# Top-32 attention and two MLPs on one core: soft-masked tiles by one VectorE pass and a ScalarE copy, the third visit on the batch's scales, another order table

## The chip, the cores and the metric

The kernel runs on one core of a Trainium2 chip. The metric is device time in microseconds of one execution, the median of several runs. The core's engines run side by side, each in its own fixed order of instructions: TensorE (PE in the profile, its weight loads PEld), VectorE (DVE), ScalarE (ACT), GpSimd (POOL) and SyncE (SP), which here issues every DMA.

## The reference

Four batches of eight heads, 576 rows, 64 columns. Attention keeps, in each row of scores, only those that are at least the 32nd largest. What comes out is laid as 2304 tokens of 512 and goes through two MLPs of 512 to 2048 to 512, the first with softplus, the second with `h - tanh(h)`.

```python
scores = scale * np.matmul(q, k.transpose(0, 1, 3, 2))
kth = np.partition(scores, -top_k, axis=-1)[..., -top_k:-top_k + 1]      # top_k = 32
scores = np.where(scores >= kth, scores, -1000000000.0)
scores = scores - np.max(scores, axis=-1, keepdims=True)
attn = np.exp(scores)
attn = attn / (np.sum(attn, axis=-1, keepdims=True) + 1e-09)
x = np.matmul(attn, v)                        # laid as 2304 x 512
g = np.maximum(h, 0.0) + np.log1p(np.exp(-np.abs(h)))   # h = x @ w_in;  x = g @ w_out
g = h - np.tanh(h)                                      # h = x @ w_in2; out = g @ w_out2
```

The inputs are float32 (moe_w_in and moe_w_out come as pairs of 32-bit words, which the kernel reads as 64-bit numbers and converts itself).

## The kernel before

**Tiles and visits.** A visit is one batch, one pair of heads and two of the four blocks of 128 query rows: four tiles of 128x576 scores. Sixteen of the 32 visits also carry a small tile with the 64 rows left over of each of the two heads, which gives 144 tiles in all. Each tile goes this way: `front` multiplies q by k on TensorE (tile name s) and ScalarE copies the scores to SBUF (ssb); `chain` finds the 32 largest by four MAX8 and three MATCH_REPLACE8 on VectorE (m, x); `exps` makes the exponentials on ScalarE; `mask`; `turn` splits the result in two f16 parts (ScalarE casts hl, GpSimd subtracts for the lower part) and transposes them by DMA (pT); `back` multiplies by v on TensorE (px), and ScalarE, VectorE and GpSimd divide by the sum (r2) and split the output (x, xs), which a DMA transposes into the MLP's input (xy). Two or three tiles' worth of buffers are there for each.

**Two ways to the exponential.** Where ScalarE holds the softplus table because the first MLP is in work, a tile is "soft": `exps` takes softplus in place of the exponential, and `mask` sets what lies under the threshold to zero. There are 59 such tiles. The other 85 take a Prelu and an Exp, which mask by themselves, and `mask` does nothing. With SOFT at 1 a soft tile's mask is a VectorE comparison into ssb (1 or 0 times 2^38) and a GpSimd product of x and ssb.

**Scales.** All operands are split into f16 pairs after a scaling by a power of two that follows from a sum of squares. The q and k of a batch are scaled by sums over the whole batch (`qk_norm`, called for batch 0 as part of tile 4's loop turn), which `visit_scales` hands out. The first OWN visits don't wait for that: `visit_norm` takes their own sums from the q and k just loaded (tile name qss), with two ScalarE squares, two one-column products on TensorE and some small VectorE operations. A visit that comes again to the same heads finds its k in a saved copy; where that copy was scaled by the visit's own sum, three more one-element VectorE operations follow.

**MLPs.** A chunk is 256 tokens (128 for the rows left over). `gemm1` multiplies by w_in (h), `act1` applies softplus or tanh on ScalarE (r) and splits the result (g; ScalarE and GpSimd), `gemm2` multiplies by w_out (y). The weights are loaded, converted and split in 32 groups during the first quarter of the run, on all engines (whi, wlo, xy as staging).

**What sets the order.** Nothing is issued while the code runs: a `Recorder` takes down every operation with a cost in ns (`price`) and what it depends on. `order` then plans: `place` is a list scheduler over the five engines with a rank for every operation, in ns; `order` starts from the program's order with a random addition (SEED, SIG), plans five times, each time with ranks from the latest starts of the plan before, and keeps the plan with the earliest end. DLAT is what the planner adds to every DMA. `idle` puts filler matmuls of 256 columns (line 564) into gaps of TensorE's plan. `run` issues all operations in the planned order, from line 567, so nearly every row of the profile has that line and is told apart by its tile.

Of the kernel before, what the change touches and what calls it, by code (L numbers as in the profile page):

```python
# [33 lines left out]
NRM = 'cccc'  # L34
EVL = 'AA'
HIC = 'AAAA'
SOFT = 1
NKT = 3
NM = 3
NQT = 2  # L40
# [2 lines left out]
RSE = 1  # L43
KE = 'P'
NQH = 1
OWN = 3
OWN0 = 0
V0 = 0
EXQ = 0
# [24 lines left out]
LT = 1  # L74
NBF = 1
NJ = 0
SEED = 34
DLAT = 1100
MRX = 60.0
LAGA = 3  # L80
LAGB = 4
# [38 lines left out]
MARGD = 0.0  # L120
MARGA = 0.0
MARGP = 0.0


class View:
# [48 lines left out]
class Recorder:  # L174
# [199 lines left out]
    def place(self, edges, count, rank, margin, ring):  # L374
# [14 lines left out]
        while True:  # L389
# [67 lines left out]
            if ring and e == "SP":  # L457
                busy = max(busy, t + 800) + o.lat
                end[i] = busy + DLAT
            for j, lat in edges[i]:  # L460
# [7 lines left out]
    def order(self, margin):  # L468

        ops = self.ops  # L470
        succ = self.link()
        self.lead = [self.shared(o) for o in ops]
        rank = [o.rank for o in ops]
        if SEED:
            draw = random.Random(SEED)
            rank = [r + draw.gauss(0.0, SIG) for r in rank]
        best = None
        for turn in range(TURNS):
            start, end, done = self.place(succ, [len(o.preds) for o in ops], rank, margin, True)
            total = max(start[o.i] + o.cost for o in ops)  # L480
            if best is None or total < best[0]:
                best = total, done, start, end
            back = [[] for _ in ops]
            for o in ops:
                for j, lat in o.preds.items():
                    back[o.i].append((j, lat + (end[j] - start[j] - ops[j].cost if ops[j].eng == "SP" else 0.0)))
            late = self.place(back, [len(x) for x in succ], [-x for x in start], {}, False)[1]
            rank = [-x for x in late]
        for o in ops:
            o.start = best[2][o.i]  # L490
        self.ends = best[3]
        return best[1]

    def idle(self, done):

# [75 lines left out]
def topk_attention_two_mlps(  # L571
# [388 lines left out]
    def visit_norm(vi):  # L960

        pair = tiny(2), tiny(2)
        (vi.sq, vi.sk), (vi.iq, vi.ik) = ([t[:, u : u + 1] for u in range(2)] for t in pair)
        vi.es, vi.nes, vi.nst = (tiny() for _ in range(3))
        both = NJ and vi.again is None
        ss = al("qss", 1, [P, 3], F32)
        left = vi.left is not None
        if vi.again is not None:
            vi.sk, vi.ik = None, vi.again[2]
        if left:  # L970
            j, st = xy_take([P, D], F16, "nst")
            xy_free.append(j)
            nc.scalar.activation(st, vi.ql, AF.Square, accum_out=ss[:, 1:2])
        for u, (t, s, inv) in enumerate(((vi.q, vi.sq, vi.iq), (vi.k, vi.sk, vi.ik))):
            if t is None:
                continue
            j, st = xy_take([P, 2 * D * t.shape[2]], F16, "nst")
            xy_free.append(j)
            nc.scalar.activation(st, t.rearrange("p j t d -> p (j t d)"), AF.Square, accum_out=ss[:, 2 * u : 2 * u + 1])
            n = 2 if u == 0 and left else 1  # L980
            if not both:
                pow2_scale(col_norm(ss[:, 2 * u : 2 * u + n], n), s, inv)
        if both:
            pow2_scale(col_norms([ss[:, 0 : 2 if left else 1], ss[:, 2:3]]), *pair)
        exp_scale(vi.iq, vi.ik, vi.es, vi.nes, vi.nst)
# [286 lines left out]
    def mask(st):  # L1272
        if st.soft and SOFT:
            nc.vector.tensor_scalar(st.s, st.s, st.m[:, 31:32], PUP, op0=ALU.is_ge, op1=ALU.mult)
            nc.gpsimd.tensor_mul(st.p, st.p, st.s)
        elif st.soft:
            nc.vector.scalar_tensor_tensor(st.p, st.s, st.m[:, 31:32], st.p, op0=ALU.is_ge, op1=ALU.mult)
            nc.scalar.activation(st.p, st.p, AF.Copy, scale=PUP)
# [193 lines left out]
    def run_gemm2(stp):  # L1472
        ch = stp.ch
        if stp.g == 0:
            acc = new_acc(ch.T)
            if stp.m == 0:
                ch.acc1 = acc
            else:
                ch.acc2 = acc
        stp.acc = ch.acc1 if stp.m == 0 else ch.acc2  # L1480
        gemm2(stp)
        if stp.g == NG - 1:
            if stp.m == 0:
                y_finish(ch)
            else:
                out_finish(ch)
# [104 lines left out]
    def prep_for(st):  # L1591
# [3 lines left out]
        if not vi.kT:  # L1595
            if i < OWN or OWN0 and vi.b == 0:
                visit_norm(vi)
# [48 lines left out]
    def next_step(n):  # L1646

        if phase[0] is None:
            can1 = c1[0] < len(order) and order[c1[0]][1] <= n
            can2 = wdone[0] == 4 * NG and c1[0] >= MINC  # L1650
            if can2 and len(kept) >= AHEAD:
                phase[0] = (kept.pop(0), 1)
            elif can1:
                ch = order[c1[0]][0]
                c1[0] += 1
                kept.append(ch)
                phase[0] = (ch, 0)
            elif can2 and kept:
                phase[0] = (kept.pop(0), 1)
            else:  # L1660
                return None
            phase[1] = 0
        (ch, m), g = phase
        phase[1] += 1
        if phase[1] == NG:
            phase[0] = None
        return ch, m, g
# [118 lines left out]
    while pend:  # L1786
        run_gemm2(pend.pop(0))
    nc.run(tc, {"PE": MARG, "DVE": MARGD, "ACT": MARGA, "POOL": MARGP})

# [29 lines left out]
```

## Time and profile before

| | |
|---|---|
| median of 3 runs | 1158.74 us (1156.74 to 1159.31) |
| the profiled execution's own time | 1160.61 us |
| its span | 1158.9 us |
| PE busy | 1015.5 us (88% of the span) |
| DVE busy | 960.0 us (83%) |
| ACT busy | 908.6 us (78%) |
| POOL busy | 870.9 us (75%) |

The page cuts the span into 40 slices. DVE's busy share is eight or nine tenths in all slices from the second to the 34th, and then falls away; PE's is between two and seven tenths in the first seven and eight or nine tenths after them, to the end. PE's granted clock is under nine tenths of full speed in the second to the eighth slice. So the two engines that carry most of the work are not short of it at the same time: the one has little to do at the end, the other at the start.

### The profile page before, as it was taken

What the parts mean: (1) busy time and instruction counts of PE and PEld (TensorE: products, weight loads), DVE (VectorE), ACT (ScalarE), POOL (GpSimd) and SP (SyncE); (2) the same over time, 40 slices, a digit from 0 to 9 for tenths busy, and PEclk for the clock granted to TensorE, in tenths of its full rate; (3) what the DMA queues carried; (4) which work ended last, traced back from release to release, by engine and by line L of the source; (5) the groups of instructions that cost most, each with busy time, mean ns of one, the idle gap of its engine ahead of it and who ended that gap; (6) DMA issues with size and microseconds to landing.
All of it is one profiled execution on the core that took longest, in us unless ns stands there. A gap on an engine that the chain in (4) does not pass through costs nothing.

```text
span 1158.9 us, 27885 instructions
## 1 busy us (share of the span) xinstructions
PE 1015.5 (88%) x9979; PEld 787.2 (68%) x9979; DVE 960.0 (83%) x2116; ACT 908.6 (78%) x1891; POOL 870.9 (75%) x1234
## 2 busy tenths in 40 slices
PE   4377542898898989999999999999998999999998
PEld 2244331687657867887689867886687779977965
DVE  4989999999998999989999999999899999510111
ACT  7899999899997988778877987798678776733422
POOL 5456899899887967967899879888796699543433
PEclk9688855899999999999999999999999999999999
DMA  9988977935689785655764754557555353200000
GB/s 308 248 268 250 274 209 211 205 104 88 128 176 221 161 181 104 147 81 108 148 149 86 154 96 105 112 105 145 125 99 132 81 107 69 48 6 19 2 9 20
DMA packets 322828, 153.17 MB, mean 132 GB/s; under 512 B 270208, under 2 KB 302464, under 8 KB 322688
## 3 DMA queue, kind: packets, MB, share of 16 engines
q1 hardware_dynamic: 322688, 151.39, 57.2%
q8 instruction: 78, 1.28, 0.5%
q14 instruction: 62, 0.51, 0.1%
HBM read 73.04 MB, written 15.37 MB: 76 GB/s over the span
## 4 chain that ended last, share of the span: by engine, by line
PE 42%; ACT 15%; POOL 13%; DVE 13%; DMA 8%; issue 7%; SPq 1%; POOLq 0%; ACTq 0%; DVEq 0%
PE y L567 19%; PE h L567 18%; DVE m L567 5%; DVE x L567 4%; POOL hl L567 4%; PE px L567 3%; ACT x L567 2%; PE s L567 2%; DMA pT<-hl 2%; POOL g L567 2%; ACT whi L567 2%; ACT ssb L567 2%; ACT r L567 2%; ACT hl L567 1%; ACT xy L567 1%
## 5 line engine op out<-in xcount | busy, mean ns | idle before, releaser
L567 PEld LDWEIGHTS <-whi 128*128 128x128 f16 x3872 | 359.5, 98 | 80.7 <-issue 23.7
L567 PE MATMUL h<-xy,whi 128*128 128x256 f16 (+1 forms) x2560 | 395.9, 263 | 10.6 <-ACT r L567 6.4
L567 PE MATMUL h<-xy,wlo 128*128 128x256 f16 (+1 forms) x1280 | 324.8, 263 | 0.0
L567 DVE MAX8 m<-x 128x8 f32<-128x576 f32 x432 | 315.2, 746 | 1.2
L567 POOL TENSOR_TENSOR hl<-x,hl 128x64 f16<-128x64 f32 (+1 forms) x288 | 214.8, 763 | 54.9 <-ACT hl L567 47.0
L567 DVE MATCH_REPLACE8 x<-m,x 128x576 f32<-128x576 f32 x288 | 212.9, 740 | 0.0
L567 PEld LDWEIGHTS <-wlo 128*128 128x128 f16 x1920 | 188.0, 98 | 21.6 <-issue 3.7
L567 PE MATMUL y<-g,whi 128*128 128x256 f16 (+1 forms) x1280 | 200.1, 262 | 1.6 <-POOL g L567 1.3
L567 PE MATMUL y<-whi,g 128*128 128x512 f16 x576 | 195.5, 380 | 0.2
L567 POOL TENSOR_TENSOR g<-r,g 128x512 f16<-128x512 f32 (+1 forms) x160 | 172.0, 1076 | 13.4 <-PE y L567 8.4
L567 PE MATMUL y<-g,wlo 128*128 128x256 f16 (+1 forms) x640 | 163.0, 262 | 0.0
L567 DVE SCALAR_TENSOR_TENSOR r<-h,hinb,r 128x512 f32<-128x512 f32 (+1 forms) x80 | 55.0, 688 | 119.5 <-ACT r L567 119.3
L567 ACT ACTIVATE x<-ssb,nb,tiny 128x576 f32<-128x576 f32 x144 | 124.4, 866 | 23.0 <-DVE m L567 16.4
L567 PEld LDWEIGHTS <-g 128*128 128x128 f16 x864 | 81.9, 98 | 72.8 <-issue 1.3
L567 PEld LDWEIGHTS <-pT 128*128 128x128 f16 (+1 forms) x2240 | 89.9, 103 | 43.6 <-issue 21.6
L567 DVE MAX8 m<-ssb 128x8 f32<-128x576 f32 x144 | 107.6, 747 | 13.8 <-ACT ssb L567 13.4
L567 PE MATMUL px<-vhl,pT 128*128 128x65 f16 (+1 forms) x2240 | 97.1, 198 | 20.3 <-DMA pT<-hl 6.7
L567 ACT CAST hl<-x 128x576 f16<-128x576 f32 x144 | 96.3, 669 | 22.1 <-POOL x L567 19.6
L567 PE MATMUL s<-kT,qT 128*128 128x288 f16 x512 | 89.1, 299 | 24.8 <-ACT ssb L567 22.8
L567 PE MATMUL y<-wlo,g 128*128 128x512 f16 x288 | 109.2, 379 | 0.0
L567 DVE MATCH_REPLACE8 x<-m,ssb 128x576 f32<-128x576 f32 x144 | 106.5, 739 | 0.0
L567 POOL TENSOR_SCALAR r<-r,gsb 128x512 f32<-128x512 f32 (+1 forms) x80 | 53.5, 669 | 59.1 <-ACT g L567 58.5
(129 smaller groups left out, 1788.8 us busy)
## 6 DMA issues: line engine op xcount, KB each, us to landing
whi<-in_moe_w_in_dram SPq DMA_DIRECT2D x8, 1024.0 KB, 5.8
wlo<-in_moe_w_in_dram SPq DMA_DIRECT2D x6, 1024.0 KB, 7.4
vd<-vhl SPq DMA_DIRECT2D x16, 330.0 KB, 3.7
vhl<-vd SPq DMA_DIRECT2D x16, 330.0 KB, 3.6
kd<-kT SPq DMA_DIRECT2D x32, 160.0 KB, 2.4
whi<-in_moe_w_out_dram SPq DMA_DIRECT2D x5, 1024.0 KB, 5.5
wlo<-in_moe_w_out_dram SPq DMA_DIRECT2D x5, 1024.0 KB, 6.3
kT<-kd SPq DMA_DIRECT2D x32, 160.0 KB, 2.7
```

The lines of the kernel that those rows point to most:

```text
L567: fn(*a, **k)
```

## The change

Three numbers and the planner's last step change. SOFT at 0 takes the other branch of `mask`, which stood in the code before: one VectorE operation compares the scores with the threshold and multiplies x by the result, and a ScalarE copy with a scale of 2^38 follows in place. OWN at 2 lets the third visit take the batch's scales. SEED and DLAT get other values, and after the five plans a table of 51 entries is applied: each adds a random number (its seed, its spread) to the rank of the operations that the kept plan starts in a stretch (from, to, in ns of the plan); the sum is planned once more and issued.

```diff
-SOFT = 1
+SOFT = 0
-OWN = 3
+OWN = 2
-SEED = 34
-DLAT = 1100
+SEED = 3
+DLAT = 1700
+SHIFTS = (
+    (51873, 627410, 687410, 400), (80903, 645783, 665783, 150), (38871, 414678, 434678, 400), (11372, 845916, 865916, 150),
...
+)
             late = self.place(back, [len(x) for x in succ], [-x for x in start], {}, False)[1]
             rank = [-x for x in late]
+        home = list(best[2])
+        rank = list(home)
+        for seed, lo, hi, sigma in SHIFTS:
+            draw = random.Random(seed)
+            rank = [r + (draw.gauss(0.0, sigma) if lo <= h < hi else 0.0) for r, h in zip(rank, home)]
+        start, self.ends, done = self.place(succ, [len(o.preds) for o in ops], rank, margin, True)
         for o in ops:
-            o.start = best[2][o.i]
-        self.ends = best[3]
-        return best[1]
+            o.start = start[o.i]
+        return done
```

Every engine's order differs from the first instructions on. Counted over the whole program, the number of instructions changes only so: DVE's 59 comparisons become 59 products, and 12 one-column operations go; POOL loses 59 products; ACT gets 59 copies and loses two squares; PE loses two one-column products and has 111 filler matmuls where there were 87 (41 ahead of the first MLP product where there were 56, 70 behind it where there were 31). The instructions of the new kernel have line 588 (fillers 585).

On SyncE, around the transposes that bring the first chunk's input (xy_0_80 from xs_130 is its last part). Before:

```order
L567 DMA_TRANSPOSE pT_123<-hl_122 128x9x128
L567 DMA_TRANSPOSE pT_126<-hl_125 128x9x128
L567 DMA vhl_133<-vd_134 128x1320
L567 DMA whi_0_71<-in_moe_w_out_dram 128x512 x2
L567 DMA_TRANSPOSE xy_0_80<-xs_127 128x2x128
L567 DMA whi_0_71<-in_moe_w_out_dram 128x512 x2
L567 DMA_TRANSPOSE pT_123<-hl_122 128x9x128
L567 DMA xy_0_98<-in_moe_w_out_dram 128x512
L567 DMA_TRANSPOSE xy_0_80<-xs_130 128x2x128
```

And now:

```order
L588 DMA_TRANSPOSE pT_123<-hl_122 128x9x128
L588 DMA_TRANSPOSE qlT_145<-zq_63 128x4x128
L588 DMA ql_140<-in_q_dram 64x64
L588 DMA_TRANSPOSE pT_126<-hl_125 128x9x128
L588 DMA_TRANSPOSE xy_0_80<-xs_127 128x2x128
L588 DMA xy_0_113<-in_moe_w_out_dram 128x512
L588 DMA xy_0_98<-in_moe_w_out_dram 128x512
L588 DMA whi_0_71<-in_moe_w_out_dram 128x512 x2
L588 DMA_TRANSPOSE xy_0_80<-xs_130 128x2x128
```

A later tile's pT transpose, which stood between the two xy transposes, stands behind them now; the weight loads ahead of them are others, in about the same number.

On GpSimd, at the first soft tiles. Before:

```order
L567 TENSOR_TENSOR x_111<-x_111,ssb_96 128x576
L567 MEMSET kraw_73 64x2x64
L567 TENSOR_SCALAR nb_124<-m_94,tiny_64 128x1
L567 TENSOR_TENSOR zq_63<-ql_140,zq_63 64x128 x2
L567 TENSOR_TENSOR x_121<-x_121,ssb_112 128x576
L567 TENSOR_TENSOR hl_125<-x_111,hl_125 128x512
L567 TENSOR_TENSOR hl_125<-x_111,hl_125 128x64
```

And now:

```order
L588 TENSOR_SCALAR nb_124<-m_94,tiny_64 128x1
L588 TENSOR_TENSOR wlo_0_72<-whi_0_71 128x512 x2
L588 TENSOR_TENSOR hl_122<-x_95,hl_122 128x64
L588 TENSOR_TENSOR hl_122<-x_95,hl_122 128x512
L588 TENSOR_TENSOR hl_125<-x_111,hl_125 128x64
L588 TENSOR_TENSOR hl_125<-x_111,hl_125 128x512
L588 TENSOR_SCALAR nb_119<-m_110,tiny_64 128x1
```

The products of x and ssb are gone, and the subtractions for hl follow each other with less between them.

On ScalarE, at the first soft tile (x_95). Before, around its cast:

```order
L567 CAST xs_127<-x_0_128 128x128
L567 COPY ssb_93<-s_92 128x576
L567 ACTIVATE x_1_131<-px_78,r_0_129 128x64
L567 ACTIVATE wlo_0_72<-wlo_0_72 128x256 x2
L567 ACTIVATE wlo_0_72<-wlo_0_72,tiny_64 128x256
L567 CAST hl_122<-x_95 128x576
L567 ACTIVATE r_1_132<-px_78,tiny_64 128x1
```

And now, around the new copy:

```order
L588 ACTIVATE px_81,ss_109<-px_81 128x128
L588 ACTIVATE wlo_0_72<-wlo_0_72,tiny_64 128x256
L588 ACTIVATE x_95<-x_95 128x576
L588 ACTIVATE wlo_0_72<-wlo_0_72,tiny_64 128x256
L588 ACTIVATE r_2_136<-px_78,tiny_64 128x1
L588 COPY ssb_93<-s_92 128x576
```

The copy of x_95 stands between two weight conversions and ahead of a step of another tile's `back` (r_2_136); the cast of the same tile follows later on ScalarE.

## Rows read from the trace of the kernel before

**Rows 1.** Four stretches: busy us (instructions) by engine, PE's clock, DMA.
```profile
core 0: us, PE busy (x) PEld busy (x) DVE busy (x) ACT busy (x) POOL busy (x), PEclk, DMA share, GB/s
0.00:223.00 223.00, 116.07 (x750) 72.55 (x751) 202.11 (x450) 206.52 (x432) 161.26 (x204) 0.73 0.90 251
223.00:450.00 227.00, 205.65 (x2046) 163.54 (x2043) 213.93 (x482) 208.81 (x469) 189.07 (x277) 0.98 0.71 149
450.00:1000.00 550.00, 539.44 (x5822) 434.18 (x5820) 523.94 (x1147) 434.83 (x894) 459.25 (x674) 1.00 0.54 111
1000.00:1159.00 159.00, 154.38 (x1372) 116.96 (x1369) 20.04 (x40) 58.47 (x98) 61.35 (x81) 1.00 0.06 16
```

**Rows 2.** Timeline of PE at the first MLP product: start, us, instruction, [idle before].
```profile
220.59 0.39 PE L567 MATMUL px<-whi,tiny 128*128 128x128 bf16 x2 [1.06 <-DVE whi L567]
...
223.03 0.38 PE L567 MATMUL h<-xy,whi 128*128 128x256 f16 x2
```

**Rows 3.** Timeline of SyncE's queue: the last transpose of the first chunk's input.
```profile
218.53 1.17 SPq L567 DMA_TRANSPOSE xy<-xs x1
```

**Rows 4.** DMA issues from 218.4 to 219.8 us: us from issue to landing last.
```profile
xy<-xs SPq DMA_TRANSPOSE x1, 5.0
```

**Rows 5.** Timeline of GpSimd, 195 to 222 us.
```profile
206.43 2.38 POOL L567 TENSOR_TENSOR x<-x,ssb 128x576 f32<-128x576 f32 x1
...
215.63 0.60 POOL L567 TENSOR_TENSOR xs<-x,xs 128x128 f16<-128x128 f32 x1
```

**Rows 6.** Groups by form: count | busy us, mean ns | idle just before, releaser.
```profile
L567 POOL TENSOR_TENSOR x<-x,ssb 128x576 f32<-128x576 f32 x59 | 85.2, 1444 | 6.0 <-DVE ssb L567 5.4
L567 DVE TENSOR_SCALAR ssb<-ssb,m 128x576 f32<-128x576 f32 x59 | 49.4, 840 | 4.1 <-ACT x L567 4.0
L567 ACT CAST hl<-x 128x576 f16<-128x576 f32 x144 | 96.3, 669 | 22.1 <-POOL x L567 19.6 <-DMA pT<-hl 1.9
L567 ACT COPY ssb<-s 128x576 f32<-128x576 f32 x144 | 91.3, 634 | 5.1 <-PE s L567 3.3 <-POOL x L567 1.0
```

**Rows 7.** Tiles ssb, vhl and xy on DVE: duration ns min/median/max, first and last start.
```profile
L567 DVE TENSOR_SCALAR ssb<-ssb,m x59: 496/636/2695, 203.7 to 981.2; 128x576 f32<-128x576 f32 x59
L567 DVE SCALAR_TENSOR_TENSOR vhl<-v,tiny,vhl x16: 857/877/2010, 29.3 to 879.5; 128x640 f16<-128x640 f32 x16
L567 DVE SCALAR_TENSOR_TENSOR xy<-xy x36: 399/494/1377, 58.9 to 273.4; 128x256 int32<-128x256 int32 x36
```

**Rows 8.** Group by form: the two-input pass over vhl.
```profile
L567 DVE SCALAR_TENSOR_TENSOR vhl<-v,tiny,vhl 128x640 f16<-128x640 f32 x16 | 16.6, 1036 | 2.7 <-ACT vhl L567 2.7
```

**Rows 9.** GpSimd's products of x and ssb by stretch: busy us (count), clock, DMA.
```profile
0.00:223.00 223.00, 5.18 (x3) 0.73 0.90 251
223.00:450.00 227.00, 16.30 (x11) 0.98 0.71 149
450.00:1000.00 550.00, 63.73 (x45) 1.00 0.54 111
```

**Rows 10.** Waits from 223 to 450 us: who, for whom, us in total, times, longest.
```profile
PEld L567 <- DMA pT<-hl: 7.1, 9, 1.9
PE h L567 <- ACT r L567: 5.8, 4, 2.8
PE px L567 <- DMA pT<-hl: 3.6, 5, 1.6
```

**Rows 11.** Timeline of PE: the last one-column product of batch 0's norms.
```profile
70.23 0.16 PE L567 MATMUL px<-tiny 128*128 128x1 bf16 x1 [0.56 <-ACT x L567]
```

**Rows 12.** Timeline of ACT, 80 to 92 us: the third visit's k.
```profile
83.52 0.72 ACT L567 ACTIVATE xy<-kraw 128x640 f16<-128x640 f32 x1
...
89.69 0.55 ACT L567 ACTIVATE khl<-kraw,tiny 128x320 f16<-128x320 f32 x1
```

**Rows 13.** Groups: the filler matmuls.
```profile
L564 PE MATMUL y<-tiny 128*128 128x256 bf16 x56 | 8.7, 311 | 0.0
L564 PE MATMUL h<-tiny 128*128 128x256 bf16 x31 | 4.8, 274 | 0.0
```

12 rows, old and new, of the table SHIFTS are left out of this document.

## The prediction

> **What bounds the kernel now.** I read the time by stretches first [rows 1]. From 450 to 1000 us PE is busy for 539.4 of 550 us and from 1000 on for 154.4 of 159, at full clock (1.00, the 2.4 GHz level): there it is full. DVE has nearly nothing left after 1000 us (20 of 159). Ahead of 223 us it is the other way round: DVE is busy for 202 of 223 us, ACT for 206.5, PE for 116. The reader is to see that 223 us is no arbitrary cut: the first product of the MLPs starts at 223.03 [rows 2], and from there PE is the bound, with 227 - 205.65 = 21.35 us of idle time to 450, 550 - 539.44 = 10.56 to 1000 and 159 - 154.38 = 4.62 behind it, the last of it for the output. So the span is
>
> 223.0 (start of the MLPs) + 899.5 (PE's work after it: 205.65 + 539.44 + 154.38) + 36.5 (its idle time) = 1159.0.
>
> None of the edits takes work from the 899.5. The time can only move by the start, by the 36.5 us of idle time and by what is added to PE.
>
> What sets the start: the last transposed part of the first chunk's input is issued at 218.53 [rows 3] and lands 5.0 us later [rows 4], as the product starts. It had waited for its split on POOL at 215.63 [rows 5]. PE's own wait of 1.06 us at 220.59, for a weight [rows 2], lies ahead of the landing and is covered.
>
> **The change, part by part.**
>
> *The masks.* For each of 59 soft tiles POOL loses 1.44 us and DVE's comparison of 0.84 us goes [rows 6]. The comparison lasted 0.50 us at its shortest, 0.64 in the middle [rows 7]: the mean is made of waiting. In its place DVE gets a pass over x, scores and threshold. No row shows it with 576 elements. Of the same operation, 256 elements took 0.399 and 640 took 0.857 us at their shortest [rows 7], which puts 576 at 0.78 (0.399 + 320 x 0.458 / 384); the mean of the second lies 0.18 above its shortest [rows 8], so with such waits 0.96. I take 0.90, between them, bounds 0.77 (0.857 x 576 / 640) and 1.18 (0.84 with the old wait of 0.34 on top): +0.06 us a tile, 3.5 in all, between -4 and +20. ACT gets a copy; the cast of as many elements takes 0.67, the copy of the scores 0.63 [rows 6]. I take 0.65, 38 us in all; nearest rows on both sides leave it between 0.55 and 0.80.
>
> Per tile the chain from the threshold to the cast gets shorter, from 0.84 + 1.44 to 0.90 + 0.65, by 0.73 us, and POOL is free for 1.44 us. Where does that count? Three masks lie ahead of 223 us, 11 between 223 and 450, 45 later [rows 9]. In the middle stretch PE and its weight loads waited 3.6 + 7.1 us for transposed tiles [rows 10]; some third of that stretch's tiles are soft (11 of about 34 casts), so 3 to 4 us of those waits can go. ACT loses there 227 - 208.8 = 18.2 us of slack [rows 1] only to 11 x 0.65 = 7.2. After 450 ACT has 115 us of slack for 45 x 0.65 = 29, and its waits of 19.6 us for POOL's product [rows 6] go.
>
> The skill has a rule that speaks against this part. The Trainium skill, SBUF — State Buffer, "Who interferes with whom": a VectorE instruction with two SBUF inputs shares a read interface with a GpSimd instruction that reads SBUF, and the second to start blocks until the first is through. By that rule the new pass gets no less lock time than the comparison, though it uses no double-port mode; the 2.01 us maximum of the two-input pass [rows 7] agrees.
>
> *The third visit.* Its own squares (0.72 us on ACT for k, at 83.52, and a shorter one for q), two one-column products on PE and 12 one-column DVE operations go, some 2 us on two engines that are both nearly full at that time. The new wait is for batch 0's scales. Their last one-column product ran at 70.23 [rows 11]; the visit's first cast of k stood at 89.69, 6.2 us behind the square [rows 12]. Behind it on ACT are the next casts and the copies of scores, which DVE waits for. With 19 us to spare the wait is hidden. If that cover went, each us of delay would go onto the start.
>
> *The order.* Read from the order: ahead of the split that ends the first chunk, POOL has one product of x and ssb less (the one of 2.38 us [rows 5]); DVE has 17 instructions less ahead of the sixteenth tile's reciprocal; SyncE has 182 rows ahead of the last xy transpose where it had 181. So DVE, POOL and PE have less ahead of the first product and the DMA queue has as much. Start: -2 us. Bounds: -4 (POOL's 2.38 and the third visit's 2 in full), +1 (a landing that takes longer behind four weight loads).
>
> The rest of the order I can't price by rows. Coarsely it is the same: the first MLP products stand behind 18 tiles' `back` products where they stood behind 19, and at no later place are they more than some 6 us of PE work apart. The planner gains nothing in PE's work; what it can gain is in the 36.5 us. Idle time from 223 to 450: -3, the waits for transposes from above; bounds -10 (half of it) and +7 (the ACT copies in full). From 450 to 1000: -1.5 of 10.56; bounds -5 and +5. Tail: 0.
>
> *Fillers.* 24 more. A filler took 13.5/87 = 0.155 us of busy time [rows 13], 3.7 us in all, nearly all inside gaps: +0.5, bounds 0 and 3.7.
>
> Sum: -2 - 3 - 1.5 + 0 + 0.5 = -6. The profiled execution took 1160.61 us, 1.7 more than its span and 1.9 more than the median; -6 gives 1154.6 for it and 1152.7 beside the median of 1158.74. I predict 1153.
>
> **The rivals.**
>
> *A. ScalarE becomes the bound in the middle stretch (slower).* Place: 223 to 450 us, where it is busy for 92% and grows to 95%. PE already waits 5.8 us there for softplus and tanh results (r) [rows 10]. If every copy stands ahead of such a result, PE waits 7.2 us more, the 3 us gained on transposes are lost, and the planner's shorter start gives back 2: 1158.7 + 7.2 - 2 + 0.5 = 1164. It decides from the point where that wait passes 5.8 + 5 = 11 us. For it: ACT is the fullest engine ahead of 223 us. Against: a product stands on PE well ahead of its use, since `gemm2` lags three steps behind. 17%.
>
> *B. The fillers tell of new holes (slower).* The planner fills only stretches that it finds mostly empty. Behind the first MLP product it now places 70 where there were 31: 21 around the 49th tile's products (8 before), 7 around the 69th (none), 12 near the last tiles (3). PE's longest single wait of the middle stretch was 2.8 us [rows 10]; three holes of that size are +8.4, the result 1158.7 + 8.4 - 6 = 1161. Against: DLAT adds 600 ns to each planned DMA, and the holes may be made of that alone. 9%.
>
> *C. DVE's pass is longer than I take it (no change).* With the full lock time it lasts up to 1.18 us; at 1.07, halfway to that from 0.96, it costs +0.23 x 14 = 3.2 us ahead of 450 us and 0.23 x 45 = 10 after, against 26 us of slack there (550 - 523.9), of which I put 3 on PE. 1152.7 + 6.2 = 1159. The rule above is this rival's: by it, lock time stays; the rows show it in some passes only. 14%.
>
> *D. The order table takes much of the idle time (faster by far).* Half of 21.35 and of 10.56, with a start 6 us earlier: 1158.7 - 16 - 6 = 1137. For it: the waits are many and short, which is what moving instructions can cure. Against: the ranks were moved within a plan of modelled costs, and DVE is busy for 95% from 450 to 1000, so that there is little room to move. 14%.
>
> **How the numbers follow.** My forecast, 1147 to 1156, has 46%; A 17, B 9, C 14, D 14. Two runs of this kernel can't tell less than 0.2%, 2.3 us, from no change. Faster by over 2.3 us: the forecast and D, 60%. Within: C and what B misses, 16%. Slower: A and the rest of B, 24%. The range leaves out half of D and the far end of A: 1141 to 1166; the forecast's own range is 1147 to 1156.
>
> **What would show it.** The first MLP product at 221 us or before confirms the start. The product on DVE between 0.78 and 0.96 us on average, POOL's busy time down by 85 us and ACT's up by some 36 confirm the masks. PE's waits for pT between 223 and 450 down by about 3 us, with its wait for r unchanged at about 6, confirm the middle; a wait for r beyond 11 us speaks for A, waits of 2 us and more near the fillers for B. I am wrong if PE's work after the start is not 899 us plus the fillers, if the third visit's casts come later than 89.7 us, or if the tail behind the last DVE work grows instead of shrinking.

## The result and the profile after

The changed kernel took 1146.99 us, median of 4 runs (1146.66 to 1151.68), beside 1159.03 for the kernel before on the same chip (1156.74 to 1164.02): a ratio of 0.9913, 95% interval 0.9884 to 0.9942. Run again later, on another chip (g0_after below), it gave 0.9921 (0.9900 to 0.9941). So it is faster, by 0.6 to 1.2%. The forecast was 1153, in a range of 1141 to 1166: by the medians the kernel gained 12.0 us where some 6 were forecast.

The execution that the first trace shows was the longest of the four, 1151.68 us with a span of 1150.0. The spans of the others are 1145.3, 1145.2 and 1144.9. That trace is read first, and the second trace beside it.

The four stretches of the first trace, cut at its own first MLP product [rows 1]:

```profile
core 0: us, PE busy (x) PEld busy (x) DVE busy (x) ACT busy (x) POOL busy (x), PEclk, DMA share, GB/s
0.00:216.50 216.50, 115.29 (x716) 69.64 (x717) 197.60 (x427) 202.16 (x420) 159.99 (x202) 0.76 0.92 254
216.50:450.00 233.50, 214.65 (x2148) 171.00 (x2146) 223.97 (x504) 223.99 (x500) 177.73 (x272) 0.99 0.71 151
450.00:1000.00 550.00, 542.12 (x5872) 439.06 (x5871) 517.10 (x1139) 463.86 (x944) 405.81 (x632) 1.00 0.56 111
1000.00:1150.00 150.00, 145.49 (x1274) 109.01 (x1271) 17.84 (x36) 50.98 (x85) 55.04 (x71) 1.00 0.05 13
```

And of the second:

```profile
0.00:215.20 215.20, 116.19 (x715) 70.64 (x716) 196.35 (x427) 202.02 (x420) 160.59 (x202) 0.73 0.92 256
215.20:450.00 234.80, 216.18 (x2167) 172.94 (x2165) 225.00 (x510) 226.00 (x505) 179.45 (x274) 0.99 0.71 150
450.00:1000.00 550.00, 543.41 (x5915) 441.06 (x5913) 515.63 (x1136) 463.27 (x944) 405.68 (x631) 1.00 0.57 111
1000.00:1146.00 146.00, 141.63 (x1211) 105.36 (x1208) 16.77 (x33) 49.21 (x81) 53.87 (x70) 1.00 0.04 11
```

Against [rows 1] the first MLP product comes 6.5 us earlier (7.8 in the second trace). PE's idle time falls from 21.35 to 18.85 us up to 450 us (18.62), from 10.56 to 7.88 up to 1000 (6.59) and stays at 4.5 after that (4.37). POOL loses 72 us of busy time and ACT gains 32.

The masks, first on DVE and ACT (duration in ns min/median/max, first and last start), then in the groups by form [rows 6, 7]:

```profile
L588 DVE SCALAR_TENSOR_TENSOR x<-ssb,m,x x59: 792/810/2649, 203.1 to 972.8; 128x576 f32<-128x576 f32 x59
L588 ACT ACTIVATE x<-x x59: 666/682/702, 205.0 to 973.7; 128x576 f32<-128x576 f32 x59
```

```profile
L588 DVE SCALAR_TENSOR_TENSOR x<-ssb,m,x 128x576 f32<-128x576 f32 x59 | 54.1, 918 | 5.4 <-ACT x L588 5.3
L588 ACT ACTIVATE x<-x 128x576 f32<-128x576 f32 x59 | 40.0, 681 | 5.5 <-DVE x L588 5.4
L588 ACT CAST hl<-x 128x576 f16<-128x576 f32 x144 | 96.5, 670 | 0.9 <-POOL r L588 0.7
```

The pass takes 0.918 us on average (taken: 0.90), at its shortest 0.792 (taken: 0.78); the copy 0.681 (taken: 0.65). The 22.1 us that ACT's cast waited, 19.6 of them for POOL's product, have become 0.9.

The start: on PE, SyncE and among the DMA issues (last column: us from issue to landing) [rows 2 to 5]:

```profile
216.49 0.38 PE L588 MATMUL h<-xy,whi 128*128 128x256 f16 x2
...
218.47 0.38 PE L588 MATMUL h<-xy,whi 128*128 128x256 f16 x2 [0.83 <-DMA xy<-xs]
```

```profile
214.44 1.17 SPq L588 DMA_TRANSPOSE xy<-xs  x1
```

```profile
xy<-xs SPq DMA_TRANSPOSE x1, 4.0
```

```profile
211.35 0.42 POOL L588 TENSOR_TENSOR xs<-x,xs 128x128 f16<-128x128 f32 x1
```

POOL's last split starts at 211.35 where it was 215.63, the transpose is issued 4.1 us earlier and lands 1.0 us sooner. The products of the three parts already there begin before it, and the fourth then waits 0.83 us. Before, the first product started ahead of the landing too (223.03 against 218.53 + 5.0 = 223.53), but the fourth came after it and waited for nothing:

```profile
222.48 0.60 PE L567 MATMUL px<-vhl,pT 128*128 128x65 f16 x14 [0.35 <-DMA pT<-hl]
...
224.01 0.38 PE L567 MATMUL h<-xy,whi 128*128 128x256 f16 x2
```

So the fourth product, 218.47 in place of 224.01, tells what the start really gained: 5.5 us, 5.1 of them the earlier landing. The other 1.0 of the 6.5 us comes back as that wait and little more.

The waits from 216.5 to 450 us [rows 10]:

```profile
PEld L588 <- DMA pT<-hl: 7.9, 8, 2.2
...
PE px L588 <- DMA pT<-hl: 5.1, 5, 1.7
```

And of the second trace, from 215.2 us on:

```profile
PEld L588 <- DMA pT<-hl: 6.3, 6, 2.0
...
PE px L588 <- DMA pT<-hl: 4.2, 4, 1.6
```

In place of 10.7 us for pT there are 13.0 in the first trace and 10.5 in the second, so the fall by 3 us that was forecast shows in neither. PE's wait for r, 5.8 us before, is 1.5 in the first and 1.8 in the second.

### The profile page after: what moved, and what is told of

It reads as the page before. It is cut to its first block, busy times and chain, and to the rows that moved or that the text cites. A ratio compares the mean times of both kernels' runs of the same rounds, so it can differ in the third digit from the quotient of the medians.

```text
span 1150.0 us, 27899 instructions
## 1 busy us (share of the span) xinstructions
PE 1017.5 (88%) x10001; PEld 788.7 (69%) x10001; DVE 956.5 (83%) x2104; ACT 941.0 (82%) x1946; POOL 798.6 (69%) x1175
## 4 chain that ended last, share of the span: by engine, by line
PE 40%; DVE 25%; ACT 13%; issue 8%; DMA 6%; POOL 6%; SPq 2%; POOLq 0%; DVEq 0%; ACTq 0%
PE y L588 18%; PE h L588 17%; DVE m L588 11%; DVE x L588 10%; ACT whi L588 3%; PE px L588 2%; PE s L588 2%; ACT x L588 2%; ACT ssb L588 2%; DMA pT<-hl 2%; ACT xy L588 2%; SPq L588 2%; POOL hl L588 1%; ACT wlo L588 1%; DVE r L588 1%
## 5 line engine op out<-in xcount | busy, mean ns | idle before, releaser
L588 POOL TENSOR_TENSOR hl<-x,hl 128x512 f16<-128x512 f32 (+1 forms) x288 | 216.0, 767 | 73.0 <-ACT hl L588 59.0
L588 POOL TENSOR_SCALAR r<-r,gsa 128x512 f32<-128x512 f32 (+1 forms) x80 | 53.5, 669 | 72.1 <-ACT g L588 68.7
```

Of the source, the lines that this page charges most:

```text
L588: fn(*a, **k)
```

## The experiments

Each was timed together with the kernel before on one chip, and the chip was not always the same: compare kernels by their ratios. "Work" is PE's busy time behind the first MLP product without the fillers; "gaps" is all that is left of the span there: idle time and the fillers that stand in it. Start, work and gaps are of the one profiled execution and add up to its span; the two traces of the same kernel (after, g0_after) differ by 1.3, 1.1 and 1.7 us.

| kernel | median us | ratio, 95% interval | start | work | gaps |
|---|---|---|---|---|---|
| before (the trace of the front) | 1158.74 | 1 | 223.0 | 894.4 | 41.5 |
| after | 1146.99 | 0.9913 (0.9884 to 0.9942) | 216.5 | 892.1 | 41.5 |
| g0_after | 1149.50 | 0.9921 (0.9900 to 0.9941) | 215.2 | 891.0 | 39.8 |
| e1_old_masks_new_order | 1177.64 | 1.0168 (1.0139 to 1.0197) | 219.2 | 898.2 | 58.1 |
| e2_new_masks_old_order | 1164.61 | 1.0059 (1.0039 to 1.0079) | 222.7 | 896.5 | 44.5 |
| e3_no_table | 1151.11 | 0.9939 (0.9916 to 0.9962) | 217.8 | 892.4 | 39.4 |
| e4_seed_dlat | 1160.72 | 1.0023 (1.0006 to 1.0039) | 221.8 | 892.4 | 45.7 |
| f1_masks_only | 1151.99 | 0.9941 (0.9919 to 0.9962) | 218.2 | 891.3 | 40.2 |
| f2_own_only | 1165.21 | 1.0045 (1.0026 to 1.0063) | 220.2 | 891.5 | 49.2 |
| f3_other_seed | 1152.84 | 0.9946 (0.9926 to 0.9965) | 222.3 | 893.3 | 35.6 |
| h2_pool_load | 1163.93 | 1.0037 (1.0022 to 1.0052) | 222.3 | 895.5 | 41.3 |
| i2_pool_scale | 1180.70 | 1.0186 (1.0165 to 1.0207) | 215.0 | 899.7 | 66.0 |
| f4_early_fill | 1150.97 | 0.9932 (0.9911 to 0.9952) | 216.5 | 898.7 | 35.7 |
| e6_no_fill | 1152.49 | 0.9947 (0.9925 to 0.9968) | 214.6 | 902.3 | 33.9 |

**The masks in a fixed order: e1 and e2.** The order of one kernel, planned for its own masks, issues the other's.

```diff
 # e1: after's plan, issued with            # e2: before's plan, issued with
-scalar_tensor_tensor(p, s, m31, p)        -tensor_scalar(s, s, m31, PUP)
-scalar.activation(p, p, Copy, scale=PUP)  -gpsimd.tensor_mul(p, p, s)
+tensor_scalar(s, s, m31, PUP)             +scalar_tensor_tensor(p, s, m31, p)
+gpsimd.tensor_mul(p, p, s)                +scalar.activation(p, p, Copy, scale=PUP)
```

> The changed kernel in its own order of instructions, but each soft tile's mask is issued as before the change: a VectorE comparison into the scores and a GpSimd product, put where the planner had the ScalarE copy. (In 6 of the 59 tiles the product reads the next tile's scores, so those rows come out other than the reference's.) Theory M, the masks' shorter chain and the freed GpSimd are worth the 4.5 us of my two idle terms: 1147 + 4.5 = 1151.5, GpSimd busy 85 us more, and ScalarE's casts of hl wait for GpSimd again (some 20 us). Theory O, the order of instructions makes the gain and the masks' engines don't matter: 1147 within 2 us.

> The kernel before in its own order, but each mask is issued as after the change: one VectorE pass and a ScalarE copy, put where the planner had GpSimd's product. Theory M: 1159 - 4.5 = 1154.5, the first MLP product still near 223 us or up to 2 us earlier. Theory O: 1159 within 2 us. If ScalarE is the tighter engine (rival A), 1159 + 7 = 1166 with TensorE waiting over 11 us for r between 223 and 450 us.

Both are slower than the kernel before, and neither theory's time came. In e2 POOL is rid of its products and ACT's cast no longer waits for them (1.8 us in all, 0.2 of it for POOL), yet nothing is gained: the start is where it was (222.7), work and gaps are 2.1 and 3.0 us longer. PE's wait for r in the middle stretch is 4.3 us, so it isn't rival A that makes e2 slow; that the order left no place on ACT for the copies fits, but isn't shown. In e1 POOL gets products where the plan has none. Its waits from 219.2 to 1000 us (who, for whom, us in total, times, longest):

```profile
ACT hl L588 <- POOL x L588: 33.2, 28, 2.9
ACT ssb L588 <- POOL x L588: 32.1, 19, 3.7
```

In the kernel before these were 19.6 and 1.0 us [rows 6]. So the masks and the order can't be priced one by one: one edit in the other's order costs, both together gain.

**The parts, each planned anew: e4, f1, f2, e3.** A new plan is a new draw of the order, since the planner starts from random additions. All have SEED 3 and DLAT 1700 and no table; f1 adds the masks, f2 the third visit, e3 both.

```diff
-SEED = 34, DLAT = 1100
+SEED = 3, DLAT = 1700        # e4, f1, f2, e3
-SOFT = 1
+SOFT = 0                     # f1, e3
-OWN = 3
+OWN = 2                      # f2, e3
```

> The kernel before with the new seed and DLAT alone (old masks, the third visit's own scales, no table): another order of the same instructions. If orders differ by little more than the measurement, 1159 within 2.5 us; if the order is a draw that is worth as much as the whole change, it lies 5 us or more to one side (1150 to 1154, or 1164 and more). Theory O expects 1154 or less if seed and DLAT carry the gain, 1159 or more if the table does.

> The changed kernel with an empty table of shifts: the same masks, scales, seed and DLAT, in the planner's own order. Theory O, the table makes most of the gain: 1155 to 1160. Theory M: 1147 + 2 = 1149. The first MLP product tells whether the table or the rest brought it from 223 to 216.5 us: later than 220 speaks for the table.

> The kernel before with SEED 3 and DLAT 1700 (that alone measured 1160.7) and SOFT 0; OWN stays 3, no table. With OWN 2 on top it measured 1151.1. Theory M, the masks carry the gain once the order is planned for them: 1150 to 1154, first MLP product at about 218, POOL's wait list without the mask. Rival O, the third visit carries it through an earlier start: 1158 to 1162, start at 221 to 222. Rival L, a plan is a draw and any edit moves it by some us: both this kernel and the one with OWN 2 alone lie off the sum of the parts by 4 us or more.

> The kernel before with SEED 3 and DLAT 1700 and OWN 2; SOFT stays 1, no table. Theory M (masks carry the gain): 1159 to 1162, start at 220 to 222, since the third visit's 2 us of work count in the start at most. Rival O (third visit carries it): 1151 to 1155 with the start at 218. Rival L (a draw): neither, and the parts do not add up within 4 us.

The masks carry the gain: 0.9941 / 1.0023 is -0.8%, some 9.5 us. The three kernels with the old masks and plans of their own lie at 1.0000 to 1.0045, all that are planned for the new masks, with nothing put on POOL in their place, at 0.9913 to 0.9947 (f3 below is one more draw), so this is more than a draw. f1 came as theory M had it, in time and start; f2's start did, its time is above all forecasts. e3 lies 2 us above theory M, and its start of 217.8 speaks against theory O. The two parts add up to 0.9963 where e3 has 0.9939, 2.8 us apart, which is under the 4 us that rival L asks for. The third visit's edit is worth nothing on top of them (0.9939 beside 0.9941) and +0.2% without them, at the edge of what can be told. SEED and DLAT alone change +0.2%. The table's share is the step from 0.9939 to 0.9913 or 0.9921: 2 to 3 us, with intervals that overlap, so its size is not settled.

**Another draw, and the changed kernel again: f3 and g0.**

```diff
 # f3: e3 with
-SEED = 3
+SEED = 4
```

> The changed kernel without its table and with SEED 4 in place of 3: the same operations, another draw of the order. Theory L, a draw of the order moves the time by as much as the table is worth: anywhere from 1145 to 1158, over 3 us from the 1151.1 of SEED 3. Rival F, the planner's five rounds level the draws out: within 2 us of 1151.1, and the table's 4 us is a gain of its own.

> The changed kernel again, unaltered, for a second profile and a time on the chip of the next three. Its first profile stood 4.7 us over the median of its runs. Theory R, that profile was an outlier in what it waited for: span near 1145, gaps of TensorE behind the first MLP product (idle and fillers together) some 5 us under the 41.5 us of the first profile. Rival S, the start or the clock differed: gaps again 40 to 43 us, start at 213 or earlier or work per matmul shorter. Time 1145 to 1150 either way.

With the same operations the start moved from 217.8 to 222.3 us, and the gaps behind it from 39.4 to 35.6; the ratios, 0.9939 and 0.9946, can't be told apart. So rival F's "within 2 us" holds, and theory L's 3 us don't show. In this pair a late start and small gaps go together: what a draw does not wait for at the start it waits for later. One pair is no rule, but it warns against adding the two terms as if they were separate. g0 fits neither theory well: its span is near theory R's, but its gaps are 39.8 where R has some 36.5, and its start of 215.2 is later than theory S has it. The 4.0 us between the two traces of this kernel are spread over the start, the work and the gaps.

**What of the masks gains: h2 and i2.** The forecast had put the gain on the shorter chain from threshold to cast. h2 keeps that chain and gives POOL a product again, for whose result nothing waits. i2 takes a step out of the chain and puts one on POOL beside it.

```diff
 # h2: e3 with                                      # i2: e3 with
 scalar_tensor_tensor(p, s, m31, p)                 scalar_tensor_tensor(p, s, m31, p)
 scalar.activation(p, p, Copy, scale=PUP)          -scalar.activation(p, p, Copy, scale=PUP)
+gpsimd.tensor_mul(s, s, s)                        +gpsimd.tensor_scalar(s, p, PUP)
                                                   -scalar.copy(hl, p);  gpsimd.tensor_sub(lo, p, hl)
                                                   +scalar.activation(hl, p, Copy, scale=PUP)
                                                   +gpsimd.tensor_sub(lo, s, hl)
```

> The changed kernel without its table (1151.1) with one GpSimd product of 128x576 more for each soft tile, ssb by ssb into ssb, issued behind the DVE pass and ahead of the subtraction for hl: GpSimd's load and the hold on ssb are as before the change, no operation waits for its result. The chain over ScalarE stays. Theory G, GpSimd's 85 us were the gain: 1158 to 1165 (with SOFT 1 and the other edits it was 1165.2). Rival H, the chain from the threshold to the cast, without GpSimd's queue in it, was the gain: 1150 to 1154. Between 1154 and 1158 both have a part.

> The changed kernel without its table (1151.1), without the ScalarE copy in place: the cast to hl takes the scale of 2^38 itself, and a GpSimd tensor_scalar by 2^38 from x into ssb stands beside it, from which the subtraction takes its input. ScalarE loses 40 us, the chain one step of 0.68 us, GpSimd gets some 42 us. Theory H (the chain counts): 1145 to 1150, faster than 1151.1. Theory G (GpSimd's load counts): half of the 14 us comes back, 1155 to 1159. If ScalarE, at 96% between 216 and 450 us, was the bound: 1143 to 1148.

h2 came out in theory G's range: it decides against the chain and for POOL. Its groups by form:

```profile
L574 ACT CAST hl<-x 128x576 f16<-128x576 f32 x144 | 96.4, 669 | 1.1 <-DMA pT<-hl 0.8
L574 POOL TENSOR_TENSOR ssb<-ssb 128x576 f32<-128x576 f32 x59 | 68.8, 1165 | 10.8 <-DVE x L574 10.2
L574 DVE SCALAR_TENSOR_TENSOR x<-ssb,m,x 128x576 f32<-128x576 f32 x59 | 60.0, 1019 | 3.7 <-ACT x L574 3.7
```

The cast waits for nothing, as in after, and yet with 68.8 us more on POOL all of the gain is gone: 1.0037 beside 0.9939. That the cast no longer waits 19.6 us for POOL was therefore worth nothing by itself; what counts is that the product isn't on POOL. It costs there in three ways: it takes time from the rest of POOL's queue (the split of the tiles, of the weights and of g), it holds ssb longer, and it slows the pass on DVE (below). The second is small as a wait:

```profile
ACT ssb L574 <- POOL ssb L574: 0.7, 2, 0.4
```

That is all that ACT's copies of scores waited for the product up to 1000 us, though the plan was made with the hold in it. The first and the third aren't told apart. The loss of 9.5 us of span against e3 lies in the start (+4.5), the work (+3.1) and the gaps (+1.9); the start is as late in f3 without the product, so that part can be the draw's.

The pass on DVE grew from 0.916 us in e3 to 1.019 beside the product. Over 59 passes that makes 6 us of DVE's time. Means alone don't show whose doing it is, since a few long passes move them: f3 has 0.985 and e2 1.028 without any product. The middle one of the 59 does: 0.890 in h2 and 0.895 in i2, which have one more operation on POOL for each tile, and 0.809 to 0.819 in all the others with this pass. The Trainium skill (SBUF — State Buffer, "Who interferes with whom") states that a VectorE instruction with two SBUF inputs shares its second read interface with a GpSimd instruction that reads SBUF; the medians agree with that.

i2 misses all its forecasts. Its new operation was planned at 0.71 us and took 1.64 at its shortest:

```profile
L574 POOL TENSOR_SCALAR ssb<-x x59: 1638/1648/2236, 212.0 to 1008.6; 128x576 f32<-128x576 f32 x59
```

Its waits from 450 to 1000 us:

```profile
ACT ssb L574 <- POOL hl L574: 28.3, 22, 3.6
DVE m L574 <- ACT ssb L574: 26.6, 23, 4.6
```

ssb is free only when POOL is through, ACT's next copy of scores waits for that, and DVE for the copy. So what the waits show here is the hold on ssb, other than in h2; and the plan was made with a wrong price. The size of i2's loss proves little.

**The fillers: f4 and e6.**

```diff
 # f4: after, no filler behind the first MLP product (70 less); e6: KEEP = 0, none at all (111 less)
-if y.start > WARM and y.start - end[x.i] > 300:
+if WARM < y.start < 215000 and y.start - end[x.i] > 300:
```

> The changed kernel without the 70 filler matmuls behind the first MLP product; the 41 ahead of it stay, the order is the same otherwise. Theory N, the fillers stand in gaps that end for another reason, so that PE's extra 2.8 us of work was taken from idle time: 1146 to 1148, idle time behind the start up by some 10 us (70 x 0.15). Rival P, they delay what follows them: 1138 to 1144. Rival C, they hold the clock: granted clock behind the start under 0.97 somewhere, and the time 1150 or more.

> The changed kernel without any filler matmul (111 less). Theory N: fillers ahead of the first MLP product hold PE's clock there (0.76 of full with them), but PE is busy for only 115 of 216 us in that stretch, so the start moves by no more than 2 us: 1145 to 1149. Rival C, the clock falls in the first stretch to under 0.7 and the products that DVE waits for come later: start at 219 or later, 1150 or more. Rival P, fillers delay: 1138 to 1144.

Neither is faster than after; by the ratios they are 1 to 4 us slower, with intervals that overlap. Stretch 216 to 300 us of after, of f4 and of e6:

```profile
216.00:300.00 84.00, 75.77 (x799) 65.15 (x798) 81.21 (x193) 82.05 (x188) 60.66 (x87) 1.00 0.52 110
```

```profile
216.00:300.00 84.00, 74.06 (x768) 63.60 (x766) 81.18 (x192) 81.87 (x187) 60.42 (x87) 0.96 0.50 110
```

```profile
216.00:300.00 84.00, 72.74 (x756) 62.66 (x755) 80.28 (x191) 81.08 (x184) 59.60 (x86) 0.95 0.51 107
```

With the fillers the granted clock is 1.00 there (in the second trace too), the 2.4 GHz level throughout; without them 0.96 and 0.95, so part of it went at 1.2 GHz, and the same work takes 898.7 and 902.3 us in place of 892.1. The place can be seen: in f4 PE is busy for 0.59 of the 4 us from 276 on, where the fillers make it 2.95 in after, and the clock is 0.85 in these 4 us, 0.50 in the next four and back at 1.00 from 288; in after it is 1.00 throughout. Fillers are not all that keeps the clock: f2 and i2 have theirs, and 0.97 and 0.96 in the 84 us behind their start. Most of the longer work lies in what would have been gaps: from the start on f4 takes only 0.9 us more than after, and 3.6 more than the second trace. So in f4 rival C was right about the clock and the time, theory N about the cover in part (the idle time grew by 4.0 us, not by 10). In e6 rival C was wrong: without fillers the clock ahead of 216 us is 0.72 (0.76 and 0.73 with them), and the start, 214.6, came no later.

## Why the prediction was right, and where not

**The sum.** -6 was forecast for the profiled execution, -8.9 came (1160.61 to 1151.68), and -12.9 of span in the second trace; by the medians it is -12.0, twice the forecast, inside a range that was wide enough for no change as well. The direction and what bounds the kernel were right: the time moved with the start and with PE's idle time. That single terms came near their sizes is luck in part, as their causes did not hold.

**Start, -2 (bounds -4 and +1): -6.5 and -7.8.** The term was too small and its bound too tight. The bound counted POOL's 2.38 us and the third visit's 2 us, the instructions that go. Such a count doesn't give the start: e2 drops the POOL products in the old order and starts at 222.7; f2 has the third visit's edit and starts at 220.2; f3, with all edits but the table, starts at 222.3 by another draw. The start is a property of the whole order, and over the kernels planned without the product on POOL it ran from 215 to 222 us (f1, the new masks alone, 218.2 against e4's 221.8). The landing gave another 1.0, where the bound had only a longer one. And what set the start was read too narrowly: before, the landing at 223.53 had half a microsecond to spare for the fourth product, and the first stood behind products of another tile that had waited for their pT; in after it is the landing that is waited for.

**Idle time to 450, -3: -2.5 (-2.7 in the second trace); to 1000, -1.5: -2.7 (-4.0).** The sizes held, the cause did not. The step was "the waits for transposes": PE's waits for pT down by about 3, for r unchanged at 6. It came otherwise: pT +2.3 (-0.2 in the second trace) and r -4.3 (-4.0). And h2 shows that the chain of 0.73 us, on which the step rests, gains nothing by itself. What counts is the other half of the same sentence, POOL free for 1.44 us a tile, which the prediction didn't price by itself, and only in an order that is planned for it (e2).

**Fillers, +0.5 (0 to 3.7).** In the traces PE's filler time behind the start rose from 5.1 to 10.2 us, but f4 shows that this is no cost: without them the kernel isn't faster. That the clock falls in one gap without them was in no term.

**PE's work, taken as fixed.** Without the fillers it fell from 894.4 to 892.1 and 891.0 us; from 223 to 450 the clock was 0.98 before, and 0.99 here [rows 1].

**The third visit, 0.** Its k is cast at 82.69 us (89.69 before [rows 12]); the wait is hidden, and f1 beside e3 shows that nothing that can be measured hangs on it.

**POOL -85, ACT +36.** -72 and +32: POOL's other operations took longer (the product's 85.2 us went in full, the nb rows rose from 58.4 to 63.8), and ACT's took less (its copies alone are 40.0 us).

**The rivals.** A is refuted: ACT is busy for 96% of the middle stretch, fuller than forecast, and PE's wait for r fell. B: there are more fillers, but idle time and fillers together stayed at 41.5 us, and are 39.8 in the second trace, so they tell of no new holes. C: the pass's mean is 0.918, against the 1.07 from which this rival decides, though single ones took 2.65; in h2, beside more work on POOL, it is 1.019. D asked for half of the idle time up to 1000 us; of 31.9 us 5.2 went (6.7 in the second trace).

**Open.** By which waits POOL's load reaches PE was not followed to an end; it spreads over the start, the clock and many short waits, and differs from draw to draw. How much of h2's loss is the slower pass on DVE, or the hold on ssb in the plan, was not tried; and h2 is one plan.

## What to carry to other kernels

An engine that is busy for 75% and for which the bound engine hardly waits can still set the time: taking 59 operations off its queue was worth 9.5 us, and putting a like number back, with nobody waiting for them, cost 11. This holds where the order is planned anew: in the old order the same masks gained nothing. Where a planner sets the order, price an edit by planning with and without it and not by the instructions that it moves, and compare several draws before a few us are put down to one. Ask of filler work what the clock does without it before it is counted as a cost.

## What the runs showed of the hardware

- The GpSimd tensor_scalar by 2^38 on 128x576 in float32 took 1.64 us at its shortest and 1.67 on average (i2), more than the product of two tiles (1.44 on average, [rows 6]) or of a tile with itself (1.165, h2). It isn't so of every tensor_scalar: in the same trace those on r, 128x512, took 0.70 to 0.73 on average. What makes the difference was not tried.
- The two-input pass on DVE has a floor of 0.79 us for 576 elements in every trace that has it. Its median is 0.81 to 0.82, and 0.89 to 0.90 with one more POOL operation for each tile (h2, i2); its mean runs from 0.895 (f1) to 1.028 (e2) without one, and is 1.019 and 1.095 with one.
- Without fillers the granted clock fell to 0.50, the 1.2 GHz level, for some microseconds behind a gap from 276 us on in which PE did nearly nothing (f4, e6); over the stretch of 84 us that makes 0.95 to 0.96.
